# A ring of result buffers extended into spent input rows, and a history load cut from 112 to 102 partitions

## The chip, the cores and the metric

The kernel runs on one core of one Trainium2 chip. The metric is device time in microseconds (us), the median of the runs shown; lower is better. Beside it stands one profiled execution, from which all durations in this document come.

## The reference

The input `x` is 8 sequences of 3264 rows of 192 channels. First a causal convolution of 7 taps, with taps that are a softmax of a small weight and differ by head (8 heads of 24 channels). Then a spectral mixer: 64 Fourier modes of the convolved sequence are multiplied by complex 192x192 matrices, transformed back to `y`, and a gated channel product follows.

```python
def reference(x, weight, w_r, w_i, w_ch):
    w = softmax(weight, axis=-1)                      # (8 heads, 7 taps)
    c = einsum('hk,bskhg->bshg', w, windows_of_7(x))  # causal, zeros ahead of the start
    X = rfft(c, axis=1)[:, :64]
    Y = einsum('bmd,mde->bme', X, w_r + 1j * w_i)     # other modes are zero
    u = c + irfft(Y, n=3264)
    return u + maximum(u @ w_ch, 0.0)
```

## The kernel before, in words

The eight sequences are handled as four pairs `q` = 0 to 3. `xall[128, q, 2, 26, 192]` holds, in bf16, first the rows of `x` and then, in the same place, the convolved rows `c`. Row pairs are laid out so that one "item" is 256 rows of a pair of sequences (two slots `a` = 0, 1 of 128 rows each).

**Loading.** GpSimd (POOL) issues every load of `x` with a cast from float32 to bf16: `load_unit` (L157) brings 128 partitions x 4 blocks x 192 channels at a time, 48 such transfers; `load_rest` (L166) brings the short block at the end of each half sequence and the rows ahead of it, 4 transfers on partitions 16 to 127 (112 partitions x 4 pairs x 192). It is issued after the first ten transfers of L157. The last 96 of the 128 partitions are the block itself, and the 6 ahead of them are what the 7 taps look back on. A DVE memset (L242) zeroes partitions 0 to 15 of these blocks before the load. Tile semaphores let eight loads be in flight: each issue waits until the load eight earlier has landed. After the `x` loads, 32 loads of the mixing weights (L284) go through the same queue; from the 13th pair on they wait for a ring buffer that a mix step frees.

**First stage.** For each unit of rows: convolution as banded matmuls (L303) into PSUM, copies back to `xall` (L325, L327), a fold (L332), a partial Fourier transform (L347), and transposes of `c` into `ct` (L407, L410). After the last `x` rows come sixteen mix steps (L479) which take the weights as they land.

**Second stage** (`second_stage`). There are 52 items, 13 for each pair `q` (the first pair's items come first), so 104 slots, and six extra slots which make the weights `zw` of later pairs. For each slot TensorE forms a bank of PSUM: products of `ct` with the channel weights and products `g` of the inverse transform (all L584). ScalarE clamps it in place (`relu`, L625), TensorE adds `y` onto it (L584), VectorE adds `c` and writes float32 to a result buffer (`finish`, L643), and when both slots of an item are there SyncE (SP) issues its store (L662). The order of all these instructions on each engine is fixed when the program is built, by a small planner (`second_stage`) with assumed durations; the engines then run their lists in order and wait on semaphores.

**Result buffers.** `outs` (L103) is a ring of `NO` = 7 buffers: six in `arena`, one in `band`, used by item number modulo 7. The wait for a buffer to be free (its previous item's store has landed) is put on the first clamp of the new item, not on the add:

```python
        if n >= NO and n not in clamped:
            for name in stored[n - NO]:
                wait_for(act.ins, name, "the stores from the buffer of this item's result")
```

`known` declares that an instruction needs no wait of its own on named instructions, because another one already carries it. `freed` lists the DVE instructions that last read a bank. `restore` (L612) is a ScalarE copy that puts a product computed earlier back into a bank; `second_weights` (L507 on DVE, L508 on ScalarE) scales the six extra slots into `zw`.

Of the kernel before, what the change touches and what calls it, by code (L numbers as in the profile page):

```python
# [19 lines left out]
def kernel(  # L20
# [9 lines left out]
    nc = tc.nc  # L30
    B, S, D = x.shape
    H, KK = weight.shape
# [7 lines left out]
    P = 128  # L40
    NQ = B // 2
    HS = S // 2
    NBH = HS // (2 * P)
    RR = HS - 2 * P * NBH
    NS = 1 + 2 * NBH
    TQ = 2 + 4 * NBH
# [12 lines left out]
    def sb(name, shape, dtype):  # L59
        return pool.tile([P] + shape, dtype, tag=name, name=name)  # L60
# [4 lines left out]
    NO = 7  # L65
    OB = 2 * 2 * 2 * D
    sb("pad", [64], BF16)
    arena = sb("arena", [NWA * WGB], BF16)
    xall = sb("xall", [NQ, 2, TQ, D], BF16)
    band = sb("band", [H * 2 * P], BF16)  # L70
# [29 lines left out]
    def wbuf(g):  # L100
        return wfirst[g] if g < NWC else wring[(g - NWC) % NWA]

    outs = [a.bitcast(F32).rearrange("p (i a d) -> p i a d", i=2, a=2) for a in  # L103
            [arena[:, OB * i:OB * (i + 1)] for i in range(NO - 1)] + [band[:, 0:OB]]]
    pos = [0]

    def temp(n, dtype):
# [44 lines left out]
    def load_unit(q, b0, nb, rest):  # L152
        for t in range(2 * b0, 2 * b0 + 2 * nb):
# [2 lines left out]
                          ap=[[D, P], [HS * D, 4], [1, D]])  # L156
            nc.gpsimd.dma_start(out=xall[:, q, t % 2, k:k + 4, :], in_=src)  # L157

    def load_rest():
        p0 = 16  # L160
        for i in range(2):
            for t in range(2):
                off = (i * S + HS * (2 - t) - (P - p0)) * D
                src = bass.AP(tensor=x.tensor, offset=x.offset + off,
                              ap=[[D, P - p0], [2 * S * D, NQ], [1, D]])
                nc.gpsimd.dma_start(out=xall[p0:P, :, t, i, :], in_=src)  # L166


    wr3 = wraw.rearrange("p (h k) -> p h k", h=G4)
# [1 line left out]
                                            ap=[[G4 * KK, 4], [0, 32], [1, G4 * KK]]))  # L171
# [6 lines left out]
    for u in units[1:4]:  # L178
        load_unit(*u)
    load_rest()  # L180
    nc.vector.memset(packed, 0.0)
    nc.scalar.copy(out=bd3[:, :, PW:2 * P], in_=packed[:, 0:1].unsqueeze(2).to_broadcast([P, H, 2 * P - PW]))
# [34 lines left out]
    for g in range(4):  # L217
        for r in range(4):
            dst = bd3[32 * r:32 * r + 32, G4 * g:G4 * (g + 1), 32 * r:32 * r + PW]
# [10 lines left out]
    def table(step):  # L230
        kr = kprod.rearrange("p (t r j) -> p t r j", t=NTF, r=2)
        tr = turns.rearrange("p (t r j) -> p t r j", t=NTF, r=2)
        if step == 0:
            nc.scalar.activation(out=fsc[:, :, :, 1, :], in_=kr, func=ACT.Sin, scale=TWOPI)
            nc.scalar.activation(out=turns, in_=kprod, func=ACT.Abs)
        elif step == 1:
            nc.scalar.activation(out=fsc[:, :, :, 0, :], in_=tr, func=ACT.Sin, scale=-TWOPI,
                                 bias=halfpi[:, 0:1])
            for h in range(2):
                nc.vector.memset(ftab[64 * h:64 * h + 16, 2 * NBH:NTF, :], 0.0)  # L240
        else:
            nc.vector.memset(xall[0:16, :, :, 0:2, :].rearrange("p q t i d -> p (q t) (i d)"), 0.0)  # L242
            nc.vector.memset(yet[0:64, 1, :, :], 0.0)
            nc.vector.memset(sgn[0:64, :], 1.0)
            nc.vector.memset(sgn[64:P, :], -1.0)
# [147 lines left out]
    def c_rows(q, kk):  # L393

        if kk == 0:
            return xall[:, q, :, 0:2, :]
        k = 2 + 4 * ((kk - 1) // 2) + (kk - 1) % 2
        return xall[:, q, :, k:k + 3:2, :]
# [36 lines left out]
    for k, u in enumerate(units):  # L435
        conv_pass(*u, 0)
        if k == 0:
            table(0)
        conv_pass(*u, 1)
        if k == 0:  # L440
            table(1)
        if pend is not None:
            xtrans(pend)
            pend = None
        conv_pass(*u, 2)
        if k > len(UNITS0):
            some([next_pair()[:, 0, :]])
        conv_pass(*u, 3)
        if prev is not None:
            dft(*prev)  # L450
            if prev[3]:
                pend = prev[0]
        if k == len(units) - 1:
            lt += hand_out("left", "tr", (1, 1, 1, 1))
            trans_banks(2)
        fold(*u)
        if k == 0:
            table(2)
        prev = u
# [45 lines left out]
    def scaled(dst, srcv, engine):  # L505
        if engine == "v":
            return nc.vector.tensor_scalar(out=dst, in0=srcv, scalar1=ascale[:, 0:1], scalar2=None, op0=ALU.mult)  # L507
        return nc.scalar.activation(out=dst, in_=srcv, func=ACT.Copy, scale=ascale[:, 0:1])  # L508
# [21 lines left out]
    NZ = 8  # L530
# [22 lines left out]
    def kept_view(s, ap):  # L553
        dst, form, sizes = kept[slots[s]]
        return dst, ap.rearrange(form, **sizes) if form else ap
# [15 lines left out]
    def wait_for(inst, name, reason):  # L571
        tc.add_manual_dep(inst, name, mybir.DependencyInfo(mybir.DependencyClass.Sync,
                                                           mybir.DependencyReason.DATA), reason=reason)
# [35 lines left out]
    def restore(s):  # L609
        src, dst = kept_view(s, Z[s % NZ][:, 0:2 * D])  # L610
        held.pop(s % NZ)
        nc.scalar.copy(out=dst, in_=src)  # L612

    stored = {}
    added = {}
    freed = {}
    clamped = set()

    def known(inst, names, reason):
        for name in names:  # L620
            tc.declare_no_dep(inst, name, reason=reason)

    def relu(s):
        z = Z[s % NZ][:, 0:2 * D]
        act = nc.scalar.activation(out=z, in_=z, func=ACT.Relu)  # L625
        n, a = slots[s]
        if n >= NO and n not in clamped:
            for name in stored[n - NO]:
                wait_for(act.ins, name, "the stores from the buffer of this item's result")
        clamped.add(n)  # L630
        known(act.ins, freed.get(s % NZ, ()), "the products waited for it")

    def second_weights(s, engine):
        q, i = divmod(slots[s][1], 2)
        copy = scaled(zw[:, :, 2 * q + i, :], Z[s % NZ][:, 0:2 * D].rearrange("p (t d) -> p t d", t=2), engine)
        if engine == "v":
            freed[s % NZ] = [copy.ins.name]

    def finish(s):
        n, a = slots[s]  # L640
        q, kk = items[n]
        o = outs[n % NO]
        add = nc.vector.tensor_tensor(out=o[:, :, a, :], in0=Z[s % NZ][:, 0:2 * D].rearrange("p (i d) -> p i d", i=2),  # L643
                                in1=c_rows(q, kk)[:, a, :, :], op=ALU.add)
        known(add.ins, [x for m in range(n - NO, -1, -NO) for x in stored[m] + [added[m, a]]],
              "the clamp waited for the stores")
        added[n, a] = add.ins.name
        freed[s % NZ] = [add.ins.name]
        row = HS * ((kk - 1) % 2) + 2 * P * ((kk - 1) // 2)
        if n == len(items) - 1:  # L650

            dst = bass.AP(tensor=out.tensor, offset=out.offset + (2 * q * S + row + a) * D,
                          ap=[[2 * D, P], [S * D, 2], [1, D]])
            (nc.scalar if a else nc.sync).dma_start(out=dst, in_=o[:, :, a, :])
            return
        if (n, 1 - a) not in added:
            return
        parts = [(0, P, row)] if kk else [(16, RR // 2, S - RR), (80, RR // 2, HS - RR)]
        for p0, np_, row in parts:
            dst = bass.AP(tensor=out.tensor, offset=out.offset + (2 * q * S + row) * D,  # L660
                          ap=[[2 * D, np_], [S * D, 2], [1, 2 * D]])
            d = nc.sync.dma_start(out=dst, in_=o[p0:p0 + np_, :, :, :].rearrange("p i a d -> p i (a d)"))  # L662
            stored.setdefault(n, []).append(d.ins.name)
# [8 lines left out]
    def second_stage():  # L672
# [27 lines left out]
        while left:  # L700
# [3 lines left out]
            if waiting and waiting[0][0] <= t:  # L704
                t, s = waiting.pop(0)
                restore(s)
                ready[1][0][s] = work("a", "restore", t) + LOAD
                continue
# [22 lines left out]
            if row == 0:  # L731
                ready[1][1][s] = free[0] + TURN
            elif n is None:
                e = "va"[slots[s][1] % 2]
                second_weights(s, e)
                reopen(s + NZ, work(e, "copy", free[1] + SEEN))
            else:
                relu(s)
                ready[0][0][s] = work("a", "clamp", free[1] + SEEN) + LOAD
# [14 lines left out]
    for g, beside in enumerate((0, 1, 1, 2, 2, 2, 1, 2, 2, 2, 2, 2, 2, 2, 0, 0)):  # L754
        d = g // 2
# [62 lines left out]
```

## Time and profile before

| | |
|---|---|
| median of three runs | 179.28 us (179.26 to 180.74) |
| profiled execution, its own time | 179.65 us |
| profiled execution, span of its instructions | 177.8 us |
| TensorE matmul busy | 150.1 us, 84% of the span |
| VectorE busy | 125.9 us, 71% |
| ScalarE busy | 119.1 us, 67% |
| last `x` load lands | 60.6 us |
| last weight load lands | 107.9 us |
| first product of the second stage | 110.6 us |
| last product starts, last add ends | 172.2 us, 173.1 us |

The share of an engine over the whole span says little here, since two stages with different limits lie one behind the other: loads and first stage to about 108 us, second stage from about 110 us to the end. The chain of work that ended last, and the waits within each stage, tell what sets each. "PE" is TensorE, "DVE" VectorE, "ACT" ScalarE, "POOL" GpSimd, "SP" SyncE; a q behind the name is the engine's sequencer, which waits and issues transfers.

### The profile page before, as it was taken

How to read it: one execution, taken by the hardware profiler on the slowest of the kernel's cores; microseconds unless marked ns; L12 is line 12 of the kernel's file. 1: busy time of each engine (PE TensorE's matmuls, PEld its weight loads, DVE VectorE, ACT ScalarE, POOL GpSimd, SP SyncE). 2: the span in 40 equal slices, each digit the busy share in tenths (PEclk: the TensorE clock that was granted, in tenths of full speed). 3: DMA queues.
4: the chain of work that ended last, by engine and by line, in shares of the span. 5: the costliest groups of instructions: out<-in, count | busy, mean ns of one | idle time of the engine just before them, and what ended most of it. 6: DMA issues, size and time to landing. Idle time of an engine off the chain costs nothing.

```text
span 177.8 us, 6635 instructions
## 1 busy us (share of the span) xinstructions
PE 150.1 (84%) x2837; PEld 123.7 (70%) x2837; DVE 125.9 (71%) x245; ACT 119.1 (67%) x222; POOL 64.5 (36%) x106
## 2 busy tenths in 40 slices
PE   0053897699999999899998898999989999999970
PEld 0052795589889888678766564889979878788840
DVE  3892867646868867865545543598988879799990
ACT  6358374568686685667764651889869788788850
POOL 7977999587765584444153100000000000000000
PEclk9999699999999999999999999999999999999995
DMA  2999999999999999999999990198898798899994
GB/s 16 169 182 189 191 190 190 191 191 192 191 190 191 197 205 209 204 206 210 204 206 209 205 158 2 65 385 302 306 367 325 278 327 314 319 352 370 353 320 166
DMA packets 50594, 40.16 MB, mean 226 GB/s; under 512 B 29060, under 2 KB 50564, under 8 KB 50564
## 3 DMA queue, kind: packets, MB, share of 16 engines
q0 software_dynamic: 36208, 19.67, 80.4%
q1 hardware_dynamic: 14084, 19.87, 30.8%
q8 instruction: 22, 0.36, 0.8%
q10 hardware_dynamic: 272, 0.20, 0.3%
q14 instruction: 8, 0.07, 0.1%
HBM read 39.33 MB, written 20.05 MB: 334 GB/s over the span
## 4 chain that ended last, share of the span: by engine, by line
DMA 51%; PE 28%; POOL 10%; issue 3%; DVE 3%; ACT 1%; POOLq 0%; DVEq 0%; ACTq 0%
DMA xall<-in_x_dram 23%; PE outleft L584 14%; PE outright L584 13%; DMA arena<-in_moe_w_i_dram 13%; DMA ct<-in_moe_w_i_dram 11%; POOL xall L157 8%; DMA out_dram<-arena 5%; DVE arena L643 2%; POOL ct L284 1%; ACT outright L625 1%; POOL loose L251 1%; PE sumright L479 1%; POOL arena L284 0%; DVE mixa L507 0%; DVE ymix L765 0%
## 5 line engine op out<-in xcount | busy, mean ns | idle before, releaser
L303 PEld LDWEIGHTS <-band 128*64 128x64 bf16 x944 | 37.9, 118 | 19.7 <-ACT band L222 11.0
L584 PE MATMUL outright<-mixa,gtab 64*128 64x384 bf16 x204 | 48.0, 323 | 1.2 <-ACT outright L625 1.1
L584 PE MATMUL outleft<-mixa,gtab 64*128 64x384 bf16 x212 | 48.6, 323 | 0.4 <-DVE mixa L507 0.2
L584 PEld LDWEIGHTS <-ct 64*128 64x128 bf16 x624 | 39.9, 94 | 8.7 <-PE outleft L584 0.6
L303 PE MATMUL cvleft<-xall,band 128*64 128x192 bf16 (+4 forms) x640 | 29.8, 242 | 14.9 <-ACT band L222 11.0
L157 POOL DMA_DIRECT2D xall<-in_x_dram x48 | 35.9, 762 | 8.7 <-DMA xall<-in_x_dram 7.4
L584 PEld LDWEIGHTS <-gtab 64*128 64x128 bf16 x416 | 30.2, 94 | 5.5 <-PE outright L584 2.1
L332 DVE TENSOR_TENSOR arena<-xall 128x1536 bf16<-128x1536 bf16 (+1 forms) x28 | 22.4, 840 | 7.8 <-ACT xall L327 7.4
L327 ACT CAST xall<-cvleft 128x768 bf16<-128x768 f32 (+3 forms) x29 | 21.4, 756 | 9.7 <-PE cvleft L303 9.7
L643 DVE TENSOR_TENSOR arena<-outleft,xall 128x384 f32<-128x384 f32 x46 | 24.3, 554 | 5.1 <-PE outleft L584 4.4
L584 PE MATMUL outleft<-wa,ct 64*128 64x192 bf16 x196 | 27.7, 243 | 0.1
L625 ACT ACTIVATE outright<-outright 128x384 f32<-128x384 f32 x51 | 23.6, 477 | 5.8 <-PE outright L584 2.1
L625 ACT ACTIVATE outleft<-outleft 128x384 f32<-128x384 f32 x53 | 24.3, 476 | 4.5 <-PE outleft L584 1.4
L584 PE MATMUL outright<-wa,ct 64*128 64x192 bf16 x180 | 26.4, 243 | 0.0
L643 DVE TENSOR_TENSOR arena<-outright,xall 128x384 f32<-128x384 f32 x44 | 23.4, 554 | 1.8 <-PE outright L584 1.3
L584 PE MATMUL outleft<-wb,ct 64*128 64x192 bf16 x98 | 22.5, 243 | 0.0
L379 DVE COPY ct<-trleft 128x1024 bf16<-128x1024 bf16 (+1 forms) x19 | 12.4, 662 | 12.3 <-PE trleft L410 7.1
L584 PE MATMUL outright<-wb,ct 64*128 64x192 bf16 x90 | 20.8, 243 | 0.0
L303 PE MATMUL cvright<-xall,band 128*64 128x192 bf16 (+4 forms) x304 | 15.5, 244 | 2.2 <-DVE xall L325 1.5
L377 ACT COPY ct<-trleft 128x1024 bf16<-128x1024 bf16 x13 | 13.2, 1013 | 4.5 <-PE trleft L407 2.5
L327 ACT CAST xall<-cvright 128x768 bf16<-128x768 f32 (+3 forms) x13 | 9.8, 751 | 7.9 <-PE cvright L303 5.1
L407 PEld LDWEIGHTS <-xall 128*128 128x128 bf16 x208 | 11.7, 98 | 2.6 <-issue 0.3
(129 smaller groups left out, 205.8 us busy)
## 6 DMA issues: line engine op xcount, KB each, us to landing
out_dram<-arena SPq DMA_DIRECT2D x40, 384.0 KB, 3.6
xall<-in_x_dram POOLq DMA_DIRECT2D x48, 192.0 KB, 7.7
out_dram<-band SPq DMA_DIRECT2D x7, 384.0 KB, 3.5
ct<-in_moe_w_r_dram POOLq DMA_DIRECT2D x8, 288.0 KB, 9.0
ct<-in_moe_w_i_dram POOLq DMA_DIRECT2D x8, 288.0 KB, 10.0
arena<-in_moe_w_r_dram POOLq DMA_DIRECT2D x8, 288.0 KB, 10.6
arena<-in_moe_w_i_dram POOLq DMA_DIRECT2D x8, 288.0 KB, 11.1
out_dram<-arena SPq DMA_DIRECT2D x8, 144.0 KB, 2.5
```

Source lines behind the costliest of these rows:

```text
L157: nc.gpsimd.dma_start(out=xall[:, q, t % 2, k:k + 4, :], in_=src)
L251: nc.gpsimd.affine_select(out=dst, in_=dst, compare_op=ALU.not_equal, fill=fill, base=base, pattern=pattern, channel_multiplier=1)
L284: nc.gpsimd.dma_start(out=wbuf(g)[64 * half:64 * half + 64, :, :, :], in_=src[m0:m0 + 7:2, :, :].rearrange("m (p j) e -> p m j e", j=3))
L303: nc.tensor.matmul(o, bd3[:, h, c0:c0 + P - 1:2], xall[:, q, t, ks:ks + n, GRP * h:GRP * h + GRP], start=(main and a == 0), stop=not main, ...
L327: nc.scalar.copy(out=dst, in_=srcv)
L332: nc.vector.tensor_tensor(out=cpm[:, r, :, 0:2 * nb, :], in0=src[:, :, :, 0, :], in1=src[:, :, :, 1, :], op=op)
L377: nc.scalar.copy(out=out, in_=in_)
L379: nc.vector.tensor_copy(out=out, in_=in_)
L407: nc.tensor.transpose(o, cv[:, blk, 0:P], ident[:])
L584: m = nc.tensor.matmul((Z[s % NZ] if bank is None else bank)[:, cols], l, r, start=start, stop=stop, skip_group_check=True)
L625: act = nc.scalar.activation(out=z, in_=z, func=ACT.Relu)
L643: add = nc.vector.tensor_tensor(out=o[:, :, a, :], in0=Z[s % NZ][:, 0:2 * D].rearrange("p (i d) -> p i d", i=2), in1=c_rows(q, kk)[:, a, : ...
```

## The change

Three edits.

1. Result buffers. Six more places are made of the first pair's part of `xall` (its `c` is needed no longer once all 26 adds of that pair have been issued, which an assertion holds for item 16 on). Items 0 to 15 use the seven old buffers as before. Items 16 to 21 take the six new ones, and each later item takes the buffer whose last user lies furthest back, which makes a ring of 13. The clamp's wait now names the store of that last user.
2. Waits. Clamps and adds no longer wait by themselves for an ACT copy that wrote or read the same bank earlier (`onto`), as TensorE's product in between already waited for it.
3. Loads. `load_rest` loads partitions 26 to 127 (102 partitions) in place of 16 to 127 (112), and the memset zeroes partitions 0 to 25.

```diff
+    NX = 2 * TQ * D // OB
+    LATE = NS + 3
+    xdone = xall[:, 0, :, :, :].rearrange("p t k d -> p (t k d)")
     outs = [a.bitcast(F32).rearrange("p (i a d) -> p i a d", i=2, a=2) for a in
-            [arena[:, OB * i:OB * (i + 1)] for i in range(NO - 1)] + [band[:, 0:OB]]]
+            [arena[:, OB * i:OB * (i + 1)] for i in range(NO - 1)] + [band[:, 0:OB]] +
+            [xdone[:, OB * i:OB * (i + 1)] for i in range(NX)]]
+    place = [n % NO for n in range(LATE)] + list(range(NO, NO + NX))
+    while len(place) < NQ * NS:
+        place.append(min(range(NO + NX), key=lambda b: max(n for n, p in enumerate(place) if p == b)))
+    before = [max((m for m in range(n) if place[m] == p), default=None) for n, p in enumerate(place)]
...
+    R0 = P - RR - (KK - 1)
+
     def load_rest():
-        p0 = 16
         for i in range(2):
             for t in range(2):
-                off = (i * S + HS * (2 - t) - (P - p0)) * D
+                off = (i * S + HS * (2 - t) - (P - R0)) * D
                 src = bass.AP(tensor=x.tensor, offset=x.offset + off,
-                              ap=[[D, P - p0], [2 * S * D, NQ], [1, D]])
-                nc.gpsimd.dma_start(out=xall[p0:P, :, t, i, :], in_=src)
+                              ap=[[D, P - R0], [2 * S * D, NQ], [1, D]])
+                nc.gpsimd.dma_start(out=xall[R0:P, :, t, i, :], in_=src)
...
-            nc.vector.memset(xall[0:16, :, :, 0:2, :].rearrange("p q t i d -> p (q t) (i d)"), 0.0)
+            nc.vector.memset(xall[0:R0, :, :, 0:2, :].rearrange("p q t i d -> p (q t) (i d)"), 0.0)
...
     def restore(s):
         src, dst = kept_view(s, Z[s % NZ][:, 0:2 * D])
         held.pop(s % NZ)
-        nc.scalar.copy(out=dst, in_=src)
+        onto.setdefault(s % NZ, []).append(nc.scalar.copy(out=dst, in_=src).ins.name)
...
         n, a = slots[s]
-        if n >= NO and n not in clamped:
-            for name in stored[n - NO]:
+        if before[n] is not None and n not in clamped:
+            for name in stored[before[n]]:
                 wait_for(act.ins, name, "the stores from the buffer of this item's result")
         clamped.add(n)
-        known(act.ins, freed.get(s % NZ, ()), "the products waited for it")
+        known(act.ins, [*freed.get(s % NZ, ()), *onto.get(s % NZ, ())], "the products waited for it")
...
         if engine == "v":
             freed[s % NZ] = [copy.ins.name]
+        else:
+            onto.setdefault(s % NZ, []).append(copy.ins.name)
...
-        o = outs[n % NO]
+        assert n < LATE or len([m for m, _ in added if m < NS]) == 2 * NS
+        o = outs[place[n]]
...
-        known(add.ins, [x for m in range(n - NO, -1, -NO) for x in stored[m] + [added[m, a]]],
+        known(add.ins, [x for m in range(n) if place[m] == place[n] for x in stored[m] + [added[m, a]]],
               "the clamp waited for the stores")
+        known(add.ins, onto.get(s % NZ, ()), "the products waited for the copy")
```

No instruction is added or removed on TensorE, ScalarE, VectorE, POOL or SP, and the order on each engine stays. What differs is which buffer an add writes and a store reads, which semaphores some instructions wait for, and the shape of four loads and one memset.

More of the change, by code (lines that the diff above doesn't have):

```diff
@@ L611, in restore @@
         held.pop(s % NZ)
-        nc.scalar.copy(out=dst, in_=src)
+        onto.setdefault(s % NZ, []).append(nc.scalar.copy(out=dst, in_=src).ins.name)
     stored = {}
     added = {}
+    onto = {}
     freed = {}
```

## The prediction

> **What bounds the kernel now.** I first read the chain of work that ended last, then the waits of POOL, ACT and PE stage by stage, then what the DMA queue does in each stage.
>
> Up to 108 us the chain is loads. POOL's timeline shows their beat:
>
> ```profile
> 9.42 0.74 POOL L166 DMA_DIRECT2D xall<-in_x_dram  x1
> 10.41 0.71 POOL L166 DMA_DIRECT2D xall<-in_x_dram  x1 [0.24 <-DMA xall<-in_x_dram]
> 11.49 0.70 POOL L166 DMA_DIRECT2D xall<-in_x_dram  x1 [0.37 <-DMA xall<-in_x_dram]
> ...
> 44.15 0.74 POOL L157 DMA_DIRECT2D xall<-in_x_dram  x1 [0.30 <-DMA xall<-in_x_dram]
> 45.16 0.74 POOL L157 DMA_DIRECT2D xall<-in_x_dram  x1 [0.28 <-DMA xall<-in_x_dram]
> 46.20 0.74 POOL L157 DMA_DIRECT2D xall<-in_x_dram  x1 [0.29 <-DMA xall<-in_x_dram]
> ```
>
> Columns: start, duration, idle before and its releaser. Each issue waits for the load eight earlier, so the beat is that of the landings: 1.03 us for 128 partitions x 4 = 512 packets, 32 on each of 16 DMA engines, or 32.3 ns a packet. The four L166 loads themselves land at 17.29, 18.20, 19.11 and 20.02 us: 0.91 us each for 28 packets an engine, 32.5 ns. So the engines run back to back, and one of them ends each load: the sixteen completions of the last weight load spread over 3.1 us, with the slowest engine 1.03 us behind the next. What that engine gets more or less of moves the end of the loads (107.88 us) one for one, and the chain goes on from there:
>
> ```profile
> 97.85 10.02 DMA arena<-in_moe_w_i_dram
> 107.88 0.04 issue
> 107.92 0.49 PE sumright L479 x8
> ```
>
> From 110.6 us PE is the bound. Windows of 2 us (PE, PEld, DVE, ACT, POOL busy; clock; DMA share; GB/s):
>
> ```profile
> 128.00:130.00 2.00, 2.00 (x39) 1.84 (x35) 1.74 (x5) 1.93 (x5) 0.00 (x0) 1.00 0.92 334
> 130.00:132.00 2.00, 1.41 (x24) 0.96 (x22) 1.40 (x4) 0.91 (x3) 0.00 (x0) 1.00 1.03 383
> 140.00:142.00 2.00, 1.82 (x32) 1.35 (x28) 1.77 (x4) 1.61 (x4) 0.00 (x0) 1.00 1.03 383
> 142.00:144.00 2.00, 1.71 (x27) 1.10 (x23) 1.22 (x3) 1.41 (x5) 0.00 (x0) 1.00 0.65 201
> ```
>
> PE is full but for three holes. The chain shows what two of them waited for, and ACT's timeline the third:
>
> ```profile
> 126.23 4.69 DMA out_dram<-arena
> ...
> 131.01 0.48 ACT outright L625
> ...
> 139.50 3.52 DMA out_dram<-arena
> ...
> 143.11 0.48 ACT outright L625
> ```
>
> ```profile
> 140.27 0.47 ACT L625 ACTIVATE outleft<-outleft 128x384 f32<-128x384 f32 x1 [0.77 <-DMA out_dram<-arena]
> ```
>
> A clamp waits for the store from its item's buffer, and TensorE's list, being in order, stands behind it. The span ends with the last adds (173.1 us) and their stores.
>
> **The change, part by part.**
>
> *Ring of 13.* The instruction lists put the three stalled clamps on items from 16 on. Two of them now wait for stores issued well before (one that landed at 135.7 us, for the clamp that stalled until 143.1), the first for no store at all; 39 clamps instead of 45 carry a store wait. In the steady part (156 to 170 us) eight slots take 4.58 us, so an item 1.145 us; seven items make 8.0 us between two uses of a buffer, thirteen 14.9 us. A store takes 3.4 us (median) to 4.7 us to land, so 6.9 us of added distance exceeds every lateness seen (at most 0.96 us). Price, from the distance between successive matmul starts on PE: 0.83 us at 130.7, 0.50 at 140.3 and 0.61 at 143.0, less the 0.08 to 0.16 us that the matmul ahead of each hole needs with two row tiles side by side: 0.75 + 0.34 + 0.45 = 1.5 us. What is late next: PE itself. DVE, the next candidate, is busy 36.07 of 43 us from 111 to 154, and the stores move 384 KB per 1.145 us, where back to back they have landed 0.95 us apart. A hole of 0.43 us at 152.3 has no store behind it (the clamp waits for PE) and stays. Bounds: 0.8 us if half of it returns as other waits; 1.8 us, all that PE lost in 130 to 132 and 140 to 144 against full rate. I take 1.5, since the steady part shows PE full with these same durations.
>
> Stores and adds that use `xall` instead of `arena` have the same shapes, 128x384 (0.55 us an add). Three adds now wait for an earlier DVE instruction, long done: nothing. The first store from `xall` waits for ACT too; behind it on SP are only stores, and what it waits for lies in the first stage: nothing.
>
> *Waits dropped.* Eight clamps lose a wait on ACT and eight adds lose one; three ACT copies gain one. An extra wait shows as an event instruction ahead of the clamp, median 17 ns, 49 of them on ACT. Some eleven fewer are 0.2 us at most, on ACT with 6.7 of 43 us idle in 111 to 154: nothing, and 0.2 us if that slack were gone.
>
> *Memset.* 1.34 us at 18.9 us on DVE for 16 partitions; 26 partitions have the same 1536 words each. Nothing waited for it: nothing.
>
> *102 partitions.* The number of POOL instructions stays, four of 0.71 us; on that queue the 38 later `x` loads and all weights stand behind them. In bytes the four loads shrink by 10/112 of 0.91 us each: 4 x 0.081 = 0.33 us. But every load in this trace has 128, 112 or 64 partitions, all multiples of 16, and the beats fit whole rows per engine (8 and 7). 102 rows have no sixteen equal shares. Three ways to hand them out, each at 32.4 ns a packet, four packets a row:
> - 7 rows to each engine until they run out: fourteen engines keep their 28 packets, one gets 16, one none. Nothing for the fourteen; if the slowest engine is one of the last two, the next slowest decides, 1.03 us earlier.
> - the largest number of equal shares, 6 of 17 rows, taken in turn round the engines: 24 shares on 16 engines, so eight get two (136 packets against 112, +0.78 us) and eight get one (68, 1.4 us less). If the slowest is in the heavier half, +0.78; if not, an engine 1.05 us behind it plus 0.78 ends the loads: 0.27 us earlier.
> - the same six shares always on the same engines: 4 x 68 = 272 packets against 112, +5.2 us.
>
> [...]
>
> Bounds: -1.03 and +5.2 us. I take +0.3, midway between the even split (-0.33) and the uneven one with shares in turn (+0.78), because rows are handed out whole at every beat seen.
>
> *Sum.* 179.65 - 1.5 + 0.3 = 178.45 us for the profiled execution. It stands 0.37 us above the median, so against the median: 179.28 - 1.2 = 178.1 us.
>
> **Rivals.**
> - A, slower: the six engines are always the same. They then run 5.2 us behind through the weights, each mix step waits for them, and the end moves with it: 179.28 - 1.5 + 5.2 = 183.0 us. It decides once the imbalance passes 1.5 us, some 46 packets on the slowest engine. For it: engines run back to back to 107.9 us, so nothing catches up. Against: it needs the same engines four times.
> - B: the holes come back. DVE is busy 16.52 of 17 us from 154 to 171, so if it is DVE that paces there, time won earlier is met again by adds that free banks late. Taking back two thirds leaves 0.5 us: 179.28 - 0.5 + 0.3 = 179.1. Against: in 154 to 171 PE is busy all the time, and no matmul waits for an add there.
> - C: the slowest engine is relieved (7 rows each, it among the last two) and the whole of the lost PE time returns: 179.28 - 1.8 - 1.0 = 176.5. Against: it needs one particular engine of sixteen.
> - D, the waits were not on buffers and the change does not remove them: 179.28 + 0.3 = 179.6. Against: two of the three stand in the chain with the very store. I count it with B.
>
> **How the numbers follow.** Forecast 0.58, A 0.15, B with D 0.14, C 0.13. One per cent is 1.8 us (177.5 and 181.1), about what a measurement of this kernel can tell from no change. The forecast's own spread is -1.8 + (-0.33) to -0.8 + 0.78, 177.2 to 179.3; about a quarter of it, 0.13, lies under 177.5. Faster: 0.13 + 0.13 = 0.26. Slower: A and a little for worse shares, 0.16. Same: 0.58. The range reaches from 176.9, which takes in part of C, to 181.0, which leaves out A.
>
> **What would show it.** Right: no wait of a clamp on a store; PE full in 128 to 146 us (windows at 2.00), the second stage from first product to last add 1 to 1.8 us shorter than 110.6 to 173.1. Loads: the last weight lands between 107.6 and 108.7 us, and the rest loads' landings are uneven. Wrong: last weight load beyond 110 us (A); new waits of PE or ACT on DVE (B); last weight before 107.2 (C). If the second stage keeps its three holes, the first step is wrong.

## The result, and the profile after

The changed kernel takes 178.93 us (median of 20 runs, 178.31 to 179.59); the kernel before, run beside it, 179.99 us (20 runs, 179.25 to 180.96). The ratio is 0.9937, 95% interval 0.9919 to 0.9955. In a second round of runs it was 0.9952 (0.9923 to 0.9981). So it is faster by about 1 us, well under 1%. The profiled execution took 178.36 us with a span of 176.5 us, against 179.65 and 177.8.

The small sum hides two larger parts of opposite sign. The chain of work that ended last, around the last weight load (start, duration, what):

```profile
98.23 10.27 DMA arena<-in_moe_w_i_dram
108.50 0.04 issue
108.54 0.46 PE sumright L490 x10
```

The load that was there at 107.88 us now lands at 108.50: the loads got slower by 0.62 us in this execution. The second stage runs from its first product at 111.23 us to the end of its last add at 171.73 us: 60.50 us, where it was 110.61 to 173.10, 62.49 us. It got shorter by 1.99 us. And 0.62 - 1.99 = -1.37 us, against -1.29 us in the profiled executions' own times. In windows of 2 us (PE, PEld, DVE, ACT, POOL busy; clock; DMA share; GB/s):

```profile
130.00:132.00 2.00, 2.00 (x39) 1.78 (x36) 2.00 (x5) 1.62 (x4) 0.00 (x0) 1.00 0.46 164
140.00:142.00 2.00, 2.00 (x37) 1.76 (x35) 1.91 (x5) 1.72 (x5) 0.00 (x0) 1.00 0.98 361
142.00:144.00 2.00, 2.00 (x36) 1.61 (x32) 1.74 (x4) 2.00 (x7) 0.00 (x0) 1.00 0.91 286
152.00:154.00 2.00, 2.00 (x39) 1.65 (x38) 2.00 (x5) 1.54 (x4) 0.00 (x0) 1.00 0.88 320
```

The three holes are gone, and no engine waits for an `out_dram` transfer between 111 and 174 us any more. The fourth hole, at 152.3 us, which the prediction let stay, is gone as well. The last of the windows above is full; before the change it was this one, with 1.81 us:

```profile
152.00:154.00 2.00, 1.81 (x32) 1.36 (x28) 1.43 (x3) 1.62 (x4) 0.00 (x0) 1.00 1.02 375
```

The four short loads at the front went the other way. POOL's timeline, then the table of DMA issues (count, KB each, median us to landing), then the queue of POOL (packets, MB, share of 16 engines). In the last two the first line is before, the second after:

```profile
9.42 4.29 POOL L177 DMA_DIRECT2D xall<-in_x_dram  x4
```

```profile
xall<-in_x_dram POOLq DMA_DIRECT2D x4, 168.0 KB, 7.7
xall<-in_x_dram POOLq DMA_DIRECT2D x4, 153.0 KB, 8.9
```

```profile
q0 software_dynamic: 36208, 19.67, 80.4%
q0 software_dynamic: 38768, 19.62, 82.3%
```

One such load is smaller, 153 KB, but an issue takes 1.07 us (4.29 / 4). They land at 18.80, 19.58, 20.38 and 21.44 us, unevenly. The last full load that is undisturbed ahead of them landed at 15.01 us, so the fourth comes 6.43 us behind it; before, it was 15.35 and 20.02, so 4.67 us. The engine that ends the loads has lost 1.76 us. The queue holds 38768 packets where it held 36208, though four loads with 10 rows of 4 packets less each should have taken 160 packets away: by the trace's packet sizes, 4112 of its packets are now 4 bytes long, where there were 1392.

### The profile page after: what moved, and what is told of

The parts are those of the page before. It is cut to its first block, busy times and chain, and to the rows that moved or that the text cites. A ratio compares the mean times of both kernels' runs of the same rounds, so it can differ in the third digit from the quotient of the medians.

```text
span 176.5 us, 6624 instructions
## 1 busy us (share of the span) xinstructions
PE 151.2 (86%) x2837; PEld 125.6 (71%) x2837; DVE 126.4 (72%) x245; ACT 119.4 (68%) x222; POOL 65.8 (37%) x106
## 3 DMA queue, kind: packets, MB, share of 16 engines
q0 software_dynamic: 38768, 19.62, 82.3%
## 4 chain that ended last, share of the span: by engine, by line
PE 59%; DMA 15%; DVE 12%; POOL 8%; issue 2%; ACT 1%; POOLq 0%; DVEq 0%
PE outleft L595 13%; PE outright L595 11%; PE cvleft L314 10%; DMA xall<-in_x_dram 9%; POOL xall L166 6%; DMA arena<-in_moe_w_i_dram 6%; DVE arena L658 5%; PE cvright L314 5%; PE sumright L358 4%; DVE xall L658 4%; PE trleft L418 4%; PE sumright L490 3%; PE trleft L421 3%; PE trleft L595 1%; PE cvleft L418 1%
## 5 line engine op out<-in xcount | busy, mean ns | idle before, releaser
L314 PEld LDWEIGHTS <-band 128*64 128x64 bf16 x944 | 40.0, 122 | 18.7 <-ACT band L233 11.0
L314 PE MATMUL cvleft<-xall,band 128*64 128x192 bf16 (+4 forms) x640 | 31.5, 250 | 13.8 <-ACT band L233 11.0
L658 DVE TENSOR_TENSOR arena<-outleft,xall 128x384 f32<-128x384 f32 x34 | 17.9, 553 | 2.9 <-PE outleft L595 2.6
L314 PE MATMUL cvright<-xall,band 128*64 128x192 bf16 (+4 forms) x304 | 16.2, 249 | 2.6 <-DMA xall<-in_x_dram 1.4
L658 DVE TENSOR_TENSOR arena<-outright,xall 128x384 f32<-128x384 f32 x26 | 13.7, 552 | 0.8 <-PE outright L595 0.4
```

The costliest lines, as they stand in the source:

```text
L314: nc.tensor.matmul(o, bd3[:, h, c0:c0 + P - 1:2], xall[:, q, t, ks:ks + n, GRP * h:GRP * h + GRP], start=(main and a == 0), stop=not main, ...
```

## The experiments

**The ring alone.** Everything of the change but the row count:

```diff
-    R0 = P - RR - (KK - 1)
+    R0 = 16
```

> The ring of 13 and the dropped waits alone; the four loads keep 112 partitions. Theory: the ring is worth the 2.0 us by which the second stage got shorter, and the 102-partition loads gave 0.6 us of it back. Then the last weight lands near 107.9 us, first product to last add takes 60.5 us, and the time is 1.7 to 2.2 us under before (ratio 0.988 to 0.991). Rival: the later end of the loads was chance and the row edit costs nothing; then the time equals that of the whole change (ratio 0.994).

It took 177.48 us (6 runs, 176.84 to 179.18), ratio 0.9873 (0.9824 to 0.9922). The second stage is 60.51 us long and has no holes, and the last weight lands at 107.82 us, where it was before the change. So the ring's part, 2.4 us between medians and 1.98 us in the stage, is larger than the whole change's gain, and the row count takes some of it back. This version beats the kernel before and, in the second round below, the whole change.

**The rows alone.** The kernel before, with only the load and the memset changed:

```diff
-        p0 = 16
+        p0 = P - RR - (KK - 1)
```

> The kernel before with the four loads on 102 partitions and the memset on 26, nothing else. Theory (six shares of 17 rows taken in turn, and 4-byte packets on the engines without a share): the slowest engine ends the four loads 0.8 to 1.8 us later, the last weight lands 0.3 to 1.5 us later than 107.9 us, the second stage keeps its holes (62.5 us), and the time is 0.3 to 1.5 us over before. 38768 packets on the GpSimd queue. Rival, bytes alone: 0.33 us under before. Rival, always the same six engines: 5 us over.

181.68 us (6 runs, 180.94 to 183.62), ratio 1.0112 (1.0058 to 1.0166): the row edit by itself costs 1.75 us between medians (181.68 - 179.93). From the last full load to the fourth short one it is 6.28 us (15.63 to 21.91), 1.6 us more than with 112 partitions. Its profiled execution was the slowest of its runs: its last weight landed at 110.33 us, and in its second stage clamps wait for stores as they did before (engine, line, what it waited for: us in total, times, longest):

```profile
ACT outright L625 <- DMA out_dram<-arena: 2.8, 3, 1.8
```

That stage is 64.31 us long in this execution, so part of its extra time is longer store waits, not loads. How much of the 1.75 us between medians is that, is not shown.

**The waits.** The ring with 112 partitions, with the two uses of `onto` taken out again:

```diff
-        known(act.ins, [*freed.get(s % NZ, ()), *onto.get(s % NZ, ())], "the products waited for it")
+        known(act.ins, freed.get(s % NZ, ()), "the products waited for it")
...
-        known(add.ins, onto.get(s % NZ, ()), "the products waited for the copy")
```

> As ring_112, but the clamps and adds keep the waits on ACT copies that the change dropped. Theory: these waits cost nothing, since ACT and DVE have them met already: same time as ring_112 within 0.2 us and the same 60.5 us. Rival: they cost some 20 ns each on a paced engine and more where they hold it: 0.3 us or more over ring_112.

177.12 us (6 runs, 176.85 to 178.41), ratio 0.9862 (0.9815 to 0.9909), second stage 60.51 us. The dropped waits were worth nothing that shows.

**How many buffers.** The ring with 112 partitions and eight buffers in place of thirteen:

```diff
-    NX = 2 * TQ * D // OB
+    NX = 1
```

> As ring_112, but only one buffer more: a ring of 8 in place of 13. Theory: one buffer more adds 1.15 us between two uses, the clamps were at most 0.96 us late, so seven tenths or more of the 2.0 us comes (second stage 60.5 to 61.1 us). Rival: without the holes the stores are issued closer together and land later, so that a ring of 8 still stalls; less than half of the gain (second stage over 61.5 us).

180.15 us (12 runs, 179.18 to 181.4), ratio 1.0014 (0.998 to 1.0047). My theory, that one buffer brings most of the gain, fell, and the rival's time came out. The stage is 63.28 us long, and holes of 0.97 and 1.94 us between matmuls stand at 137.08 and 146.40 us. ACT's timeline:

```profile
137.52 0.86 ACT L637 ACTIVATE outright<-outright 128x384 f32<-128x384 f32 x2 [1.22 <-DMA out_dram<-arena]
```

```profile
147.81 0.47 ACT L637 ACTIVATE outright<-outright 128x384 f32<-128x384 f32 x1 [2.05 <-DMA out_dram<-xall]
```

Items don't end in the order of their numbers. By the instruction lists, the clamp at 147.81 waits for the 27th store of SP's list with seven buffers, but for the 28th with eight. That one was issued at 142.59 us and took 5.15 us to land, until 147.73. One buffer more moved the wait to a later store. What counts at this clamp is how far back its particular store stands in SP's list, not the number of buffers. So ten were tried:

```diff
-    NX = 2 * TQ * D // OB
+    NX = 3
```

> As the ring of 13 with 112 partitions, but with three places of the first pair's rows in place of six: 10 buffers. Theory: what a buffer has to outlast is the landing of its last store (3.4 us at the median, 5.3 us at the longest) plus the two or three items by which items end out of order; at 1.145 us an item, ten buffers are 11.5 us from use to use, which is enough: second stage 60.5 to 60.9 us long, no hole over 0.3 us before a store wait, ratio 0.986 to 0.990. Rival: with any ring short of 13 the later issued stores of the new places are still waited for, as with 8 buffers: stage 62 us or more, ratio 0.996 to 1.002.

177.67 us (6 runs, 176.74 to 178.09), ratio 0.9858 (0.9818 to 0.9898), stage 60.50 us, no wait for a store in it. Ten are as good as thirteen, as far as this shows.

**Who paces the last third.** In after's chain the last 17 us are VectorE's adds, back to back, though TensorE is full as well. So which of them? The ring with 112 partitions, with the last pair's adds half as wide:

```diff
+        w = D // 2 if q == NQ - 1 else D
-        add = nc.vector.tensor_tensor(out=o[:, :, a, :], ...
+        add = nc.vector.tensor_tensor(out=o[:, :, a, 0:w], ...
```

> The ring of 13 with 112 partitions; the adds of the last pair's items (26 of 104) take 96 channels in place of 192, so half of that pair's sums are left out. TensorE, ScalarE, the stores and the order stay. Question: who paces the last third. If VectorE does (its adds run back to back from 154 us, 0.572 us each, against some 0.56 us of TensorE a slot), the stage ends earlier by the tail (the last add alone, about 0.25 us) and by some 0.01 us for each of the 26 to 30 slots, 0.3 us, so 0.5 to 0.7 us in all: stage 59.8 to 60.0 us against 60.5. If TensorE does, only the tail goes: 60.2 to 60.3 us. If ScalarE's clamps or the bank turn round pace it, more: the adds free banks earlier, but TensorE has no idle time to use it.

The stage is 60.30 us long, against 60.51. The last add alone is 0.20 us shorter (0.36 for 0.56 us), so only the tail went. DVE's timeline shows the adds back to back in the whole change (the first line, two adds in 1.13 us), and at the same pace of 0.57 us in this kernel (the three lines below it), where each add waits for TensorE:

```profile
160.54 1.13 DVE L658 TENSOR_TENSOR xall<-outleft,xall 128x384 f32<-128x384 f32 x2
```

```profile
160.39 0.36 DVE L659 TENSOR_TENSOR xall<-outleft,xall 128x192 f32<-128x192 f32 x1 [0.22 <-PE outright L595]
160.96 0.36 DVE L659 TENSOR_TENSOR xall<-outright,xall 128x192 f32<-128x192 f32 x1 [0.21 <-PE outleft L595]
161.53 0.36 DVE L659 TENSOR_TENSOR xall<-outright,xall 128x192 f32<-128x192 f32 x1 [0.21 <-PE outleft L595]
```

TensorE paces the last third; VectorE merely has no time to spare. The chain can put it on VectorE because the two are within 0.01 us a slot of each other. (The median was 176.59 us, ratio 0.9799 (0.9749 to 0.9848); of the 0.9 us by which the span of its profiled execution is shorter, 0.6 us lie after the last add, in the last stores, which this theory does not speak of.)

**The row count, varied.** On the ring of 13, 104, 113 and 96 partitions (96 leave out the six rows that the taps look back on):

```diff
-    R0 = P - RR - (KK - 1)
+    R0 = 24        # 15 and 32 in the other two
```

> The ring of 13 and the dropped waits stay; the four rest loads bring 104 partitions (24 to 127), the memset zeroes partitions 0 to 23. Theory of equal shares: 104 rows go out in the largest number of equal shares that is at most sixteen, 8 shares of 13 rows (52 packets of 384 bytes), taken in turn round the sixteen engines, and each engine without a share gets as many packets of 4 bytes in its place, about 7 ns each. Two loads then make one round: after four loads every engine has 104 real packets (before 112: -8 x 32.4 ns = -0.26 us) and 104 small ones (+0.75 us), so the fourth load lands about 0.5 us later, counted from the last full load ahead of the rest loads, than with 112 partitions, against 1.6 to 1.8 us later with 102. The queue holds 37744 packets in all (36208 - 4 x 448 + 4 x 16 x 52). Time about 0.5 us above the ring with 112 partitions: ratio about 0.990 (0.986 to 0.994). Rival 1: the small packets cost nothing, then -0.26 us. Rival 2: the same eight engines every time, then 208 packets against 112 on each, +3.1 us. Rival 3: eight rows or fewer on each engine, then no 4-byte packets are added and the queue holds 36080 packets.

> The ring of 13 stays; the four rest loads bring 113 partitions (15 to 127), one row more than before the change, and the memset zeroes partitions 0 to 14. 113 is a prime. Theory of equal shares: one share of 113 rows, so 452 packets on one engine a load and 452 small ones on each of the fifteen others; in turn round the engines, four engines have one such load each: 452 real packets against 112 (+340 x 32.4 ns = +11.0 us) and 1356 small ones (about 7.2 ns each, +9.8 us), so the end of the loads and the time go up by some 21 us, to about 198 us; the queue holds 63344 packets (36208 - 4 x 448 + 4 x 16 x 452). Rival 1: small packets cost nothing, +11 us. Rival 2: the same engine each time, +55 us. Rival 3: rows are dealt out eight to an engine with a rest, then at most one row more an engine, 0 to +0.5 us.

> The ring of 13; the four rest loads bring 96 partitions (32 to 127), and the memset zeroes partitions 0 to 31. Left out are the six rows ahead of the block, so the rows whose taps look back on them are computed with zeros. 96 rows are sixteen shares of 6 rows: 24 packets an engine in place of 28, no packets of 4 bytes added, 35952 packets in the queue. From the last full load ahead of the rest loads to the fourth rest load: 16 packets fewer, 0.52 us less than the 4.66 us of 112 partitions, so 4.15 us, against 6.4 us with 102. Time 0.5 us below the ring with 112 partitions. Rival: rows of the loads cost by something else than packets (a fixed time for each load), then no gain over 112.

The queue of POOL with 104, 113 and 96 partitions, in this order:

```profile
q0 software_dynamic: 36464, 19.62, 81.3%
```

```profile
q0 software_dynamic: 63344, 19.78, 75.4%
```

```profile
q0 software_dynamic: 35952, 19.57, 80.9%
```

- 96 partitions: packets as expected, none of 4 bytes added; the fourth short load lands 4.13 us behind the full one (15.18 to 19.31; 4.15 expected), and the last weight at 107.31 us. 177.12 us (4 runs), ratio 0.9828 (0.9783 to 0.9873). So fewer bytes brought the fourth short load 0.53 us closer here, with rows that divide evenly: in every profile with 112 partitions that distance is 4.65 to 4.68 us. Whether this lasts to the end is not shown: the kernels with 112 partitions land their last weight between 107.02 and 107.91 us, and one of them has the same median of 177.12 us.
- 104 partitions: my working was wrong, the theory of equal shares not. The largest divisor of 104 up to sixteen is 13, not 8. With 8 rows (32 packets) on each of 13 engines and 32 packets of 4 bytes on each of the other three, the count is -4 x 32 real packets and +4 x 3 x 32 small ones, 36208 + 256 = 36464, which is the first of the three lines. The distance from the full load to the fourth short one is 4.28 us (16.37 to 20.65), 0.38 us less than with 112; if the shares go round the engines in turn, an engine that got three shares out of four has 16 packets fewer and 32 small ones more, an estimated -0.3 us. But 52 shares on 16 engines would also give four engines all four shares, 16 packets more, +0.5 us. The measured -0.38 us fits only if none of these four ended the loads; the last engine stood 0.52 us behind the next at the full load, and the trace doesn't name the engines. 177.88 us (4 runs), ratio 0.9878 (0.9833 to 0.9924); its last weight lands at 108.70 us, but the full load ahead, too, was about 1 us later here than before the change.
- 113 partitions: 63344 packets, as expected to the packet, but 214.29 us (one run) where 198 was expected. Two of the loads land at 30.34 and 35.71 us. One share is 452 x 32.4 ns = 14.6 us, so they ran side by side on different engines. If the 5.4 us between them are the 452 small packets on the second one, those took 12 ns each. What the expectation lacked is the issue, in POOL's timeline:

```profile
9.43 8.28 POOL L177 DMA_DIRECT2D xall<-in_x_dram  x2
30.70 4.10 POOL L177 DMA_DIRECT2D xall<-in_x_dram  x1 [13.00 <-issue]
36.02 4.10 POOL L177 DMA_DIRECT2D xall<-in_x_dram  x1 [1.21 <-issue]
```

An issue with sixteen times 452 packets takes 4.1 us, and the third one stood still for 13 us, until the first load had landed. The fourth began 0.3 us after the second had landed, at 35.71 us. So the four loads ran two by two, not all four side by side, and the fourth landed at 57.93 us. For what these issues waited, the profile doesn't say.

Over the five row counts, the packets of POOL's queue fit these equal shares: 6 for 102 rows (38768 packets), 13 for 104 (36464), 1 for 113 (63344), and sixteen, with no packets added, for 112 (36208) and 96 (35952). On which engines the shares lie, the trace doesn't say.

**The price of the rows on one chip.** The ring with 112 partitions and the whole change, both once more:

> The ring of 13 and the dropped waits with 112 partitions, run on the same chip and against the same runs of the kernel before as the whole change, so that the price of the 102 partitions is read from medians of one chip. Ratio about 0.987 as in its first run.

> The whole change (102 partitions) on that same chip. If what the profiles show at the fourth rest load, 1.6 to 1.8 us on the slowest engine, stays to the end of the loads in most executions, it is 1 to 2 us above the ring with 112 partitions; if the term of the prediction was right, 0.3 us above it; if the later loads make it good, as the last weight of the profiled execution (0.6 us later) suggests, about 0.6 us.

177.49 us (6 runs, 177.05 to 178.37) and 179.23 us (12 runs, 178.35 to 180.0), ratios to the kernel before 0.9858 (0.9815 to 0.9901) and 0.9952 (0.9923 to 0.9981). The rows cost 1.74 us. In the profiles the last weight lands at 107.91 and 109.17 us, and the second stage is 60.50 us long in both.

## Why the prediction was right, and where it was not

The forecast was 178.1 us, 1.2 us below the kernel before; measured are 178.93 us, 1.06 us below the kernel that ran beside it. The sign, the size and the three holes are as foretold, but that the sum came out is luck: two of its terms were off in opposite directions, the ring by 0.5 to 0.9 us and the rows by 1.4 us.

- *Ring of 13, forecast -1.5 us, measured -1.99 us in the stage and about -2.4 us between medians* (177.48 against 179.93, and 177.49 against 179.84). The step that failed is "a hole of 0.43 us at 152.3 has no store behind it and stays". ACT's timeline of before had named TensorE:

```profile
152.21 0.47 ACT L625 ACTIVATE outright<-outright 128x384 f32<-128x384 f32 x1 [0.48 <-PE outleft L584]
```

  But the lists give this clamp a wait for a store, and that store, issued at 148.00 us, landed at 152.13, 0.08 us before the clamp began; at the other three holes, too, the clamp begins 0.08 or 0.09 us after its store landed. TensorE was done earlier: in the changed kernel the same clamp begins right after a product has ended which, before the change, ended at 151.65 us, 0.56 us ahead of the clamp. So the releaser in brackets was the wrong one. With it the holes are 0.75 + 0.34 + 0.45 + 0.35 = 1.89 us, close to 1.99. That is also why the gain passed the prediction's bound of 1.8 us and the "1 to 1.8 us shorter" that would have shown it right: both counted three holes. The rest between stage and medians, some 0.4 us, lies within the intervals.
- *"6.9 us added distance exceeds every lateness seen"*: the conclusion holds, the yardstick does not. The same reasoning makes eight buffers enough (1.145 us against 0.96), and with eight the stage was 63.28 us: a buffer more can put a clamp behind a later store, and without the holes stores take longer to land (median 4.0 us and longest 5.6 us in the changed kernel, against 3.4 and 4.7 us).
- *What is late next, "PE itself"*: right, shown by the half-wide adds for the last third. That also refutes B's reason, that VectorE paces the last third.
- *Waits dropped, 0*: right, shown by the kernel that keeps them. *Memset, 0*: not tried by itself; it took 1.34 us on 26 partitions as on 16, and with 32 partitions zeroed, the kernel with 96 partitions lost nothing that shows.
- *102 partitions, forecast +0.3 us, measured +1.74 us* on one chip, and 1.75 us alone. What was measured fits the second of the three ways, six shares in turn round the engines: the packet counts (38768 with 102 rows) fit six shares alone, and the same six engines each time would have cost 5.2 us by the estimate, where the fourth short load came 1.76 us later. When the forecast was made this way was a supposition; no load before the change had such a row count. I chose a value between it and an even split, "because rows are handed out whole at every beat seen"; beats of loads that divide evenly could not tell. And even this way was priced too low, since it counts only the real packets of the heavier engines, 24 x 32.4 ns = 0.78 us. The queue also holds 4112 - 1392 = 2720 more packets of 4 bytes, which is 10 engines x 68 x 4 loads: as many as if each load put one wherever an engine has no share. A heavier engine would then do two real shares and 136 small packets; 1.76 - 0.78 = 0.98 us makes them 7 ns each, if the engine that ended the loads is a heavier one. Averaged over its sixteen completions, the fourth short load comes 1.24, 1.30 and 1.74 us later in the three profiles with 102 partitions; with 10 real packets fewer an engine and 170 small ones more, that makes 9 to 12 ns each. The step "eight get one (68, 1.4 us less)" failed with it: in the changed kernel even the seven earliest completions come 0.5 to 0.7 us later, counted from the full load. The trace has no price for them before the change.
- *"Four of 0.71 us" on POOL*: 1.07 us each, for loads of sixteen times 68 packets instead of 28. This is not seen on the path: the next full load is issued at 13.67 us, against 13.55 before.
- *Loads, last weight between 107.6 and 108.7 us*: 108.50, inside. But the second profile of the same kernel has 109.17, outside.

Of the rivals, A asked for the same six engines each time. That did not happen: the fourth short load would then be 5.2 us late, not 1.8. C foretold that the whole of the lost PE time returns, and it did; but it also needed an engine that ends the loads earlier, and none of the sixteen completions came earlier. D fell with the holes. Why the end of the loads moves by 0.6 us in one execution and 1.3 us in another was not tried. Averaged over its sixteen completions, the last weight is 1.3 and 1.7 us later than before (105.98 us, against 107.27 and 107.68), so the 0.6 us owe something to how far the last engine happens to trail the others.

## What to carry to other kernels

Before cutting rows from a load, look at how many equal shares the new count makes (six with 102 rows, sixteen with 112 and 96, by the packet counts): ten rows fewer cost 1.74 us here, and sixteen rows fewer brought 0.5 us at the fourth short load, which no longer stands out in the time. A wait in an in-order list cost what the engine behind it lost (holes of 1.89 us on TensorE, a stage shorter by 1.99 us without them), so price a new ring by the store that each late instruction will wait for, read from the lists, not by the number of buffers. And where a sum of several edits comes out right, run the edits one by one: the change without its third edit (0.9873 and 0.9858) is better than the whole, and no other kernel here that computes the whole result is clearly better than that.

## What was not expected of the hardware

- The short GpSimd loads of 102, 104 and 113 partitions carried extra packets of 4 bytes: 2720, 384 and 27120 over four loads, where those of 112 and 96 carried no extra ones. Each count is what one such packet for every packet of a share, on every engine without a share, would make. By the estimates above they cost 7 to 12 ns each, where a real packet of 384 bytes takes 32.4 ns by the beat of the loads with 112 partitions (0.91 us for 28).
- The issue of a short load took longer the more packets it had (0.71 us for sixteen times 28, 1.07 for sixteen times 68, 4.1 for sixteen times 452), and the third load of 452 stood still for 13 us, until the first one had landed.
- With the holes gone, stores took longer to land: 4.0 us at the median and 5.6 at the longest in the changed kernel, against 3.4 and 4.7 before.
